# Attention keys in chunks of 128 and a half chunk, natural token order, and one cluster of attention work per head pair

## The chip, the cores and the metric

The kernel runs on one core of one Trainium2 chip. The metric is the device time of one execution in microseconds (us), the median of several runs. All runs quoted here are in the fast state: the medians of one kernel differ by less than 0.3% between sessions. PE is TensorE's matmul stream (the profile calls each entry of it a record), PEld its weight loads, DVE is VectorE, ACT ScalarE, POOL GpSimd, SP the sync engine, which issues nearly all the transfers here.

## The reference

Eight batches, twelve heads, 448 tokens, head dimension 64, all fp32. Then a SwiGLU feed-forward on 3584 tokens of width 768 with a hidden width of 1536.

```python
q_n, k_n = rmsnorm(q, g_q), rmsnorm(k, g_k)          # q, k, v: (8, 12, 448, 64)
attn = softmax(q_n @ k_n.T / sqrt(64))               # per head
x = (attn @ v) -> (B*S, H*D)                         # 3584 x 768
out = (silu(x @ w_gate) * (x @ w_val)) @ w_out       # w_gate, w_val 768 x 1536, w_out 1536 x 768
```

## The kernel before

Two heads make a pair; there are 48 pairs. The first 12 ("early") come before any long feed-forward stretch; the other 36 ("late") are set among the down-products of a block, 12 to a block. There are four blocks of two batches each; a block first makes its up-products (x times `w_gate` and `w_val`), then its down-products (times `w_out`). The last block has no attention in it. A planner written in Python gives each piece an engine and a guessed time, and fixes each engine's order when the kernel is built; the engines then run in order and wait for each other by semaphores.

A pair's 448 tokens are cut into four chunks of 112, with tokens 4p to 4p+3 on partition p. So q and v come as one DMA each, in pieces of 1 KB, and k as two in pieces of 256 B.

```python
BUFS = dict(
    qk=4, v=2, t=2, QT=2, KT=2, e=4, sums1=1, sums3=1, inv=1, rows=3, st=2, at=2, ss=3, rr=4, ...)

def load(name, key, src):                 # name "qk" (q or k) or "v"
    def emit():
        if src is k:
            x = take(name, key, [R, NJ, 2, D])                        # R = 112, NJ = 4, D = 64
            rows = k[b][2 * c : 2 * c + 2].rearrange("h (p j) d -> p j h d", j=NJ)
            for h in range(2):
                nc.sync.dma_start(x[:, :, h], rows[:, :, h])
        else:
            x = take(name, key, [R, 2, NJ, D])
            nc.sync.dma_start(x.rearrange("p h j d -> p h (j d)"), pair_rows(src, m))
    ...
    return add("SP", 0.9 if src is k else 0.45, when, emit, takes=[(name, key)], kb=224, early=25.0)

def square(x):                            # ACT, for the norm; x = 0 for q, 1 for k
    ...
# ... sums on DVE, the inverse root `rr` and the scaling of q into `t` on POOL ...
def transpose(x):                         # PE: 4 transposes for q, 4 for k
    for j in range(NJ):
        src = tiles["qk", (m, 1)][:, j] if x else tiles["t", m][:, 0, j]
        nc.tensor.transpose(transposed_to(x)[:, ts(j, R)], src.rearrange("p h d -> p (h d)"), ident[0:R, 0:R])

def scores(j):                            # PE: two 64x112 row tiles side by side
    for h in range(2):
        nc.tensor.matmul(st[0:R, h, 0:S], tiles["KT", m][rows, j, :], tiles["QT", m][rows]..., start=True, stop=True)
def exps(j):                              # ACT, reads `st`, writes `e`
    ...
def product(name, lhs, rhs, first, last): # PE: weighted sums and denominators, two 112x64 column tiles
    ...
```

## Time and profile before

| | before |
|---|---|
| median, three runs | 1600.94 us (1597.68 to 1601.45) |
| profiled span | 1598.5 us |
| busy PE / DVE / ACT / POOL | 1568.1 / 789.5 / 429.5 / 683.5 us |
| instructions on PE | 5376 |
| 2nd, 3rd, 4th long run of up-products starts at | 532.25, 919.38, 1306.51 us |

In the timeline of PE each block shows one long unbroken run of products with weights `ws` and stationary `xs` (line L1047 before). The starts of the second, third and fourth are marks; the distance between two marks is one whole steady block with 12 late pairs (387.13 us before). The time up to the first mark holds the early stage and block 0. The first marks of the two kernels, before and then after (start, duration, line, shapes, records):

```profile
532.25 171.54 PE L1047 MATMUL mm<-xs,ws 128*128 128x448 f32 x456
```

```profile
573.15 158.01 PE L1076 MATMUL mm<-xs,ws 128*128 128x448 f32 x420
```

### The profile page before, as it was taken

To read this page: it belongs to the slowest core of one execution; us is meant where nothing else is said; L and a number is where in the kernel's file an instruction comes from. 1 tells how busy PE (TensorE), PEld (TensorE's weight loads), DVE (VectorE), ACT (ScalarE), POOL (GpSimd) and SP (SyncE) were. 2 spreads that over 40 slices of the span, in tenths; PEclk is the share of its full clock that TensorE was granted. 3 is DMA by queue.
4 is the path that set the end of the run, shared out by engine and by line. 5 is a ranking of instruction groups with operands and counts; after the bars stand their busy time and mean duration, and the time that the engine had idled before them with its cause. 6 is when DMAs were issued, how large, how long until landed. Compare 5 with 4: busy or idle time off the path is not lost.

```text
span 1598.5 us, 14736 instructions
## 1 busy us (share of the span) xinstructions
PE 1568.1 (98%) x5376; PEld 774.8 (48%) x5376; DVE 789.5 (49%) x873; ACT 429.5 (27%) x689; POOL 683.5 (43%) x440
## 2 busy tenths in 40 slices
PE   6998999999999999999999999999999999999998
PEld 2333555544544555544444455554454445555554
DVE  3999768873554343444454533444344543343221
ACT  6774333334333001123333210103433311000000
POOL 5881356555656213335556422333665632222000
PEclk9999999999999999999999999999999999999999
DMA  5556677622331111212423121213223211111232
GB/s 166 179 162 215 212 246 250 227 83 85 99 120 47 55 59 57 82 61 65 125 76 108 42 69 40 88 55 99 76 81 114 73 59 59 40 59 40 94 109 76
DMA packets 116118, 161.90 MB, mean 101 GB/s; under 512 B 50756, under 2 KB 103236, under 8 KB 112452
## 3 DMA queue, kind: packets, MB, share of 16 engines
q1 hardware_dynamic: 106752, 149.84, 29.4%
q10 hardware_dynamic: 9284, 11.02, 2.3%
q8 instruction: 45, 0.74, 0.2%
q14 instruction: 37, 0.30, 0.1%
HBM read 132.12 MB, written 28.70 MB: 101 GB/s over the span
## 4 chain that ended last, share of the span: by engine, by line
PE 95%; DVE 1%; issue 1%; POOL 1%; ACT 1%; DMA 0%; SPq 0%; POOLq 0%; ACTq 0%; DVEq 0%
PE mm L1047 48%; PE mm L1228 25%; PE at L805 11%; PE st L747 9%; PE st L698 2%; DVE inv L849 1%; POOL rr L666 1%; ACT es L759 1%; PE mm L698 0%; DMA qk<-in_k_dram 0%; DVE xs L884 0%; POOL sums L770 0%; POOL t L679 0%; DVE gt L947 0%; DVE gt L951 0%
## 5 line engine op out<-in xcount | busy, mean ns | idle before, releaser
L1047 PE MATMUL mm<-xs,ws 128*128 128x448 f32 x2016 | 764.9, 541 | 3.8 <-DVE xs L884 3.8
L1047 PEld LDWEIGHTS mm<-xs,ws 128*128 128x128 f32 x2016 | 382.9, 191 | 381.5 <-issue 369.7
L1031 POOL TENSOR_TENSOR ws<-ws 128x384 f32<-128x384 f32 x192 | 200.1, 1053 | 445.3 <-DMA ws<-quarters 326.0
L1228 PE MATMUL mm<-ws,gt 128*128 128x384 f32 x912 | 308.0, 491 | 0.0
L759 ACT ACTIVATE es<-st,rr 112x448 f32<-112x448 f32 x384 | 212.2, 636 | 204.8 <-PE st L747 158.0
L1228 PEld LDWEIGHTS mm<-ws,gt 128*128 128x128 f32 x912 | 168.9, 190 | 136.4 <-issue 27.2
L849 DVE RECIPROCAL inv<-at 128x448 f32<-128x448 f32 x48 | 141.9, 2956 | 101.3 <-PE at L805 101.3
L666 POOL TENSOR_TENSOR rr<-ss,minus_half 112x16 f32<-112x16 f32 x48 | 151.7, 3161 | 83.0 <-DVE ss L658 81.2
L770 POOL TENSOR_TENSOR sums<-es 112x896 f32<-112x896 f32 x48 | 103.7, 2160 | 195.2 <-ACT es L759 133.8
L747 PE MATMUL st<-QT,KT 64*112 64x448 f32 x768 | 174.0, 569 | 6.4 <-ACT es L759 5.2
L773 POOL TENSOR_TENSOR sums<-sums,es 112x896 f32<-112x896 f32 x72 | 151.1, 2098 | 19.5 <-ACT es L759 15.3
L805 PE MATMUL at<-es,v 112*64 112x448 f32 x768 | 154.9, 545 | 2.7 <-DVE inv L849 2.7
L747 PEld LDWEIGHTS st<-QT,KT 64*112 64x112 f32 x768 | 60.9, 174 | 105.0 <-issue 74.3
L1065 DVE TENSOR_TENSOR s<-s,mm 128x448 f32<-128x448 f32 x96 | 59.5, 620 | 103.9 <-PE mm L1047 103.9
L1088 ACT COPY s<-mm 128x448 f32<-128x448 f32 x48 | 25.5, 532 | 293.6 <-PE mm L1047 293.5
L1300 DVE TENSOR_TENSOR rows<-part,mm 128x384 f32<-128x384 f32 x56 | 30.9, 552 | 145.8 <-PE mm L1228 130.2
L1228 PE MATMUL mm<-ws,hs 128*128 128x384 f32 x288 | 97.0, 490 | 0.0
L1065 DVE TENSOR_TENSOR wide<-s,mm 128x448 f32<-128x448 f32 x72 | 44.6, 620 | 101.4 <-PE mm L1047 101.4
L805 PEld LDWEIGHTS at<-es,v 112*64 112x64 f32 x768 | 50.9, 136 | 88.1 <-issue 77.1
L1065 DVE TENSOR_TENSOR gt<-s,mm 128x448 f32<-128x448 f32 x72 | 44.6, 620 | 88.8 <-PE mm L1047 88.8
L1152 ACT ACTIVATE wide<-gt 128x1344 f32<-128x1344 f32 x24 | 31.8, 1326 | 173.3 <-DVE gt L1065 173.3
L638 ACT ACTIVATE t<-qk 112x512 f32<-112x512 f32 x96 | 58.7, 635 | 68.3 <-DMA qk<-in_k_dram 55.0
(70 smaller groups left out, 901.8 us busy)
## 6 DMA issues: line engine op xcount, KB each, us to landing
ws<-quarters SPq DMA_DIRECT2D x48, 768.0 KB, 4.4
ws<-out_sides SPq DMA_DIRECT2D x28, 1152.0 KB, 5.2
qk<-in_q_dram SPq DMA_DIRECT2D x48, 224.0 KB, 4.2
qk<-in_k_dram SPq DMA_DIRECT2D x96, 112.0 KB, 4.0
v<-in_v_dram SPq DMA_DIRECT2D x48, 224.0 KB, 3.0
out_sides<-hs SPq DMA_DIRECT2D x42, 192.0 KB, 6.6
stage<-in_moe_w_val_dram SPq DMA_DIRECT2D x10, 768.0 KB, 6.3
gt<-in_moe_w_gate_dram SPq DMA_DIRECT2D x8, 768.0 KB, 7.0
```

Source lines behind the costliest of these rows:

```text
L638: nc.scalar.activation(tiles["t", m][:, x].rearrange("p j h d -> p (j h d)"), tiles["qk", (m, x)].rearrange("p a b d -> p (a b d)"), AF.Sq ...
L666: nc.gpsimd.tensor_tensor(out=rr, in0=tiles["ss", m], in1=minus_half, op=ALU.pow,)
L747: nc.tensor.matmul(st[0:R, h, 0:S], tiles["KT", m][rows, j, :], tiles["QT", m][rows].rearrange("p j r -> p (j r)"), start=True, stop=True,)
L759: nc.scalar.activation(e[:, h], tiles["st", (m, j)][0:R, h, 0:S], AF.Exp, scale=tiles["rr", m][:, at : at + 1],)
L770: engine.tensor_tensor(out=to, in0=before, in1=e, op=ALU.add)
L773: engine.tensor_tensor(out=to, in0=to, in1=e, op=ALU.add)
L805: nc.tensor.matmul(to[ds(D * h, D), 0:S], lhs(h), rhs[:, h], start=first, stop=last)
L849: nc.vector.reciprocal(inv, tiles[den][:, 0:S])
L1031: lambda to=to, a=a, b=b: nc.gpsimd.tensor_tensor(out=tiles[key][:, to], in0=tiles[key][:, a], in1=tiles[key][:, b], op=ALU.subtract,),
L1047: nc.tensor.matmul(into[:, 0:S], w[:, side, c, :], xs[:, side, c], start=(fresh and c == 0), stop=(c == NK - 1), skip_group_check=not fina ...
L1065: nc.vector.tensor_tensor(out=to(), in0=one(), in1=two[:, 0:S], op=ALU.add)
L1228: nc.tensor.matmul(banks[bank][:, 0:HALF], of(g), w[:, ts(g, HALF)], start=(g == 0), stop=(g == NG - 1),)
```

## The change

The intent: full use of the array for three quarters of the keys (chunks of 128, 128, 128), the last 64 keys by four 64x64 tiles at once, each for half of the queries; tokens in natural order; and the attention steps of a pair in one cluster among the feed-forward products, where many pairs had two (PE's timeline shows 21 clusters of attention in a steady block before). With it the planner's guessed times and some of its constants change, and the output goes out in whole tiles.

Parts of the edit ("..." marks a cut):

```diff
-        qk=4, v=2, t=2, QT=2, KT=2, e=4, sums1=1, sums3=1, inv=1, rows=3, st=2, at=2, ss=3, rr=4,
+        qk=4, v=2, t=2, QT=2, KT=2, e=4, eh=2, sums=1, inv=1, rows=3, st=2, at=1, ss=3, rr=4,
...
-                if src is k:
-                    x = take(name, key, [R, NJ, 2, D])
-                    rows = k[b][2 * c : 2 * c + 2].rearrange("h (p j) d -> p j h d", j=NJ)
-                    for h in range(2):
-                        nc.sync.dma_start(x[:, :, h], rows[:, :, h])
-                else:
-                    x = take(name, key, [R, 2, NJ, D])
-                    nc.sync.dma_start(x.rearrange("p h j d -> p h (j d)"), pair_rows(src, m))
...
+                x = take(name, key, [P, NJ, 2, D])
+                rows = src[b][2 * c : 2 * c + 2].rearrange("h s d -> s h d")
+                for j in range(NJ):
+                    for p in range(0, P, width(j)):
+                        nc.sync.dma_start(x[ds(p, width(j)), j], rows[ds(P * j, width(j))])
+
+            when = ready - (26.0 if name == "qk" else 16.0)
+            return add("SP", 0.9, when, emit, takes=[(name, key)], kb=256, early=25.0)
...
             for j in range(NJ):
                 src = tiles["qk", (m, 1)][:, j] if x else tiles["t", m][:, 0, j]
+                w = width(j)
                 nc.tensor.transpose(
-                    transposed_to(x)[:, ts(j, R)], src.rearrange("p h d -> p (h d)"),
-                    ident[0:R, 0:R],
+                    transposed_to(x)[:, ds(P * j, w)],
+                    src[0:w].rearrange("p h d -> p (h d)"),
+                    ident[0:w, 0:w],
                 )
...
+        for j in (3, 0, 1, 2):
+            when = (ready + 0.3 if j in (3, 0) else base) + 0.01 * (j % 3)
+            half = j == NJ - 1
             st = add(
-                "PE", 0.75, when, lambda j=j: scores(j), after=[kt, qt],
+                "PE", 0.41 if half else 0.76, when, lambda j=j: scores(j), after=[kt, qt],
                 uses=[("KT", m), ("QT", m)], takes=[("st", (m, j))],
-                group=("s", m, j // 2), mode="rows",
-            )
+                group=("c", m - 1 if j in (3, 0) else m), mode="quarters" if half else "rows",
+            )
...
+        def half_product(lhs, at):
+            e = tiles["e", (m, NJ - 1)]
+            for x in range(2):
+                for h in range(2):
+                    nc.tensor.matmul(
+                        tiles["at", m][ds(D * h, D), x, ds(at, Q)], lhs(ds(D * x, D), h),
+                        e[ds(D * x, D), h], start=False, stop=True, skip_group_check=True,
+                    )
```

`width(j)` is 128 for chunks 0 to 2 and 64 for the last, which is loaded twice, to both halves of the partitions. That makes five DMA issues for each of q, k and v, all in pieces of 256 B: 15 a pair, where there were 4.

## The prediction

> **What bounds the kernel now.** I read the busy table and the chain of waits first, to see which engine sets the time.
>
> ```profile
> PE 1568.1 (98%) x5376; PEld 774.8 (48%) x5376; DVE 789.5 (49%) x873; ACT 429.5 (27%) x689; POOL 683.5 (43%) x440
> PE   6998999999999999999999999999999999999998
> PE 95%; DVE 1%; issue 1%; POOL 1%; ACT 1%; DMA 0%; SPq 0%; POOLq 0%; ACTq 0%; DVEq 0%
> ```
>
> TensorE (PE) is busy 98% of 1598.5 us and 95% of the chain. Only the first four slices (160 us), where the first 12 head pairs are made, have holes. So after about 145 us the time is a sum of matmuls, and any PE time saved there is saved whole.
>
> Next the groups of PE instructions (line, operation, shapes, count, then busy us and mean ns), to see how much of that the change touches:
>
> ```profile
> L1047 PE MATMUL mm<-xs,ws 128*128 128x448 f32 x2016 | 764.9, 541 | 3.8 <-DVE xs L884 3.8
> L747 PE MATMUL st<-QT,KT 64*112 64x448 f32 x768 | 174.0, 569 | 6.4 <-ACT es L759 5.2 <-DVE QT L729 0.8
> L805 PE MATMUL at<-es,v 112*64 112x448 f32 x768 | 154.9, 545 | 2.7 <-DVE inv L849 2.7
> L805 PE MATMUL at<-sums,ones 112*64 112x448 f32 x240 | 53.3, 539 | 0.0
> ```
>
> Every fp32 matmul leaves two records. The mean is a latency: the step is shorter. Attention (scores, weighted sums, denominators, transposes) is some 440 us of 1568; the feed-forward products are untouched.
>
> Then the timeline of PE in one late pair (start, duration, line, shapes, records). Starts, not durations, give costs:
>
> ```profile
> 747.19 1.76 PE L747 MATMUL st<-QT,KT 64*112 64x448 f32 x8
> 748.88 3.23 PE L805 MATMUL at<-es,v 112*64 112x448 f32 x16
> 751.94 0.92 PE L805 MATMUL at<-sums,ones 112*64 112x448 f32 x4
> 752.79 1.76 PE L747 MATMUL st<-QT,KT 64*112 64x448 f32 x8
> 754.48 4.14 PE L1228 MATMUL mm<-ws,gt 128*128 128x384 f32 x12
> 758.46 0.55 PE L698 MATMUL st<-ident,qk 112*128 112x112 f32 x4
> 758.84 0.55 PE L698 MATMUL st<-ident,t 112*128 112x112 f32 x4
> 759.23 4.05 PE L1228 MATMUL mm<-ws,gt 128*128 128x384 f32 x12
> ```
>
> Four 112-column transposes take 0.383 us, so 95.75 ns each. In the chain the pure stretches are 189.42 us for 504 records of 448 columns (375.8 ns each) and 96.76 for 300 of 384 (322.5). All three equal 2 x columns / 2.4 + 2.5 ns. Scores at 747.19 take 1.69 for 8 records: two run side by side, 4 x 0.3758 = 1.503, the rest is change of array mode. Whole block check: the product stretches of two successive blocks start at 532.42 and 919.54, 387.12 apart. The order of instructions gives 252 products of 448 (x 0.7517 = 189.4), 150 of 384 (x 0.645 = 96.75), 12 pairs at 8 transposes + 4 score steps + 5 column steps (0.766 + 3.007 + 3.759 = 7.53; x 12 = 90.4), and 57 mode changes. The rest, 10.6 us / 57, is 0.186 us per change.
>
> The early stage, by windows (width, busy of PE, PEld, DVE, ACT, POOL; clock; DMA share; GB/s):
>
> ```profile
> 26.26:80.00 53.74, 50.98 (x270) 20.47 (x270) 45.26 (x38) 44.08 (x73) 43.72 (x19) 1.00 0.52 155
> 80.00:135.20 55.20, 50.47 (x248) 18.66 (x245) 50.59 (x39) 39.54 (x64) 38.42 (x22) 1.00 0.49 158
> ```
>
> PE still leads (101.5 of 108.9 us) but DVE follows at 95.9, ACT at 83.6.
>
> **What the Trainium skill says.** "TensorE: Matmul & The Clock Gate", Wait — 56ns, not 53.3ns?: warm matmuls start N / 2.4 GHz + about 2.5 ns apart. This trace agrees if fp32 counts two cycles per column and record. "TensorEngine Tiling (Array Packing)", Key Properties: going to another tiling mode drains TensorE; here 0.186 us. Same page, Gotcha 1: row tiles may not share a PSUM bank at one time; the change obeys (each query half of the output has its own bank), no run shows it. "DMA: Bandwidth & Descriptors", Specifications: line rate needs at least 512 B per transfer. The trace agrees: at 20 to 23 us 1 KB pieces move at some 370 GB/s, while the 256 B pieces of k move at about 200.
>
> **The change part by part.**
>
> 1. Keys by 128. Per late pair, before: 4 score steps, 4 value steps, 1 denominator step, each 448 wide with two tiles side by side: 9 x 0.7517 = 6.77. After: 3 full chunks of scores, 3 x 0.7517 = 2.26; the last 64 keys as four 64x64 tiles at 224 columns, two records deep: 2 x (2 x 224 / 2.4 + 2.5) = 0.378; the column steps now as two 224-wide halves, 4 x 4 x 0.1892 = 3.03; the half chunk's values 0.378. Sum 6.04, saving 0.73. I don't take all of it: twice as many weight loads (136 ns recorded for 64 columns) must hide behind matmuls half as long, and the author's own schedule now reckons 0.81 per column step and 0.41 per half. I take 0.78 and 0.40: 6.18 with 2.265 for scores, saving about 0.58. Transposes (6 of 128, 2 of 64) keep 0.767.
>
> 2. Clustering. The title suggests fewer mode changes, but the instruction order counts 64 per steady block against 57: full-mode interruptions fall, yet the four-tile mode adds two changes per pair. Cost 7 x 0.186 / 12 = 0.11 per pair. Net 0.47 x 36 late pairs = **17 us**, all on the path. (By the pure formula 22; by the author's step costs about 11.)
>
> 3. Early pairs. Before 6 column steps: 8.28 per pair with transposes; after 7.35, since both values and ones use the half chunk. 12 changes more in the stage: 0.19 per pair. PE saves 0.74 x 12 = 9 us. The second A-side product moves ahead of the one that waits for odd tokens: 2.27 us of work falls into the 2.75 us hole before 135.20. Against it: DVE work is the same, and the order even puts three more weight conversions (about 3.7 us) ahead of the last reciprocal; with 95.9 of 108.9 already used I expect new PE waits of 4 to 5 us.
>
> 4. Loads. q and v go from 1 KB to 256 B pieces, rows are 512 for 448, and a pair needs 15 DMA issues rather than 4. Issue time: k's two took 1.23 us, q 0.33, so 4.6 us per pair (estimate) against 1.9 on SP; transfer at 19 to 20 ns per 256 B (from 35 to 37 us, 885 packets under 512 B and 128 of 1 KB filled 68% of 16 engines; at 44 ns per 1 KB, from 370 GB/s, 18 ns remain for each small one, and 44 to 46 us gives 20) makes 3.7 against 2.3 us per pair. With pairs every 9 us both stay below the limit, but the first keys come about 1.2 us later. Net early gain **5 us**.
>
> 5. ACT, POOL, stores. The half chunk's exp is 224 wide: from 636 ns at 448 and 1326 at 1344 the slope gives about 0.44, so 4.7 us rather than 5.1 per pair; POOL's sums stay. Whole-tile stores halve the output DMAs; tail 0.5 us. None is on the path otherwise.
>
> 1600.9 - 17 - 5 - 0.5 = **1578.5 us**.
>
> **Rivals.** (a) Weight loading binds in the 224-wide and four-tile work. For: loads double while the stream time doesn't. Against: transposes load 128 columns every 95.75 ns though the record lasts 141, so loads pipeline. If the half chunk took twice 0.378, 0.7 us more per late pair and 1.1 early would go: about 1617, a loss; if only the column steps took 0.85, 4 x 0.07 x 48 pairs = 13 us: 1592. (b) DVE becomes the bound early: its loop (sums 1.08, reciprocal 2.95, division 0.62) sits between one pair's output and the next, because the output tile has one buffer. For: 95.9 of 108.9 us. Then early gains nothing: 1583. (c) Loads bind early, SP or DMA: landings stretch to 8.7 us beside weights already; the early stage could lose 5 us: 1588. (d) Everything fits as by formula and early waits don't grow: 1569.
>
> **Range and chances.** The late part lies between 11 and 22 us of gain, early between -3 and +10, so 1566 to 1591. Over 2% faster means below 1568.9, which needs (d) nearly whole: 0.12. Slower by 2% needs several rivals at once: 0.01. Within 2%: 0.87.
>
> **What would show it.** Steady block spacing, 387.1 now, should be about 381.5 (379.7 by formula, 383.4 by the author's costs). In the PE timeline, 16 column matmuls (32 records) should take about 3.1 us, the four-tile groups 0.4 each, changes 0.19. Early, successive weighted sums should be 8.8 to 9.2 us apart, rather than 9.5 to 10; if DVE is the releaser before them, (b) holds; if DMA or SP, (c). First continuous up-products should run from about 140 to 143 us with one product more behind them. Wrong would be: four-tile groups near 0.75, block spacing above 386, or new waits of PE in the late blocks.

## The result, and the profile after

| | before | after |
|---|---|---|
| median | 1601.08 us (1597.68 to 1601.45, 4 runs) | 1660.02 us (1657.10 to 1661.42, 4 runs) |
| ratio | | 1.0371, 95% interval 1.0350 to 1.0392 |
| profiled span | 1598.5 us | 1657.1 us |
| marks | 532.25, 919.38, 1306.51 | 573.15, 968.69, 1365.64 |
| block, from mark to mark | 387.13, 387.13 | 395.54, 396.95 |

A ratio is the mean time of one kernel's runs over the mean of the other's runs in the same rounds, so it isn't quite the ratio of the medians. The changed kernel is slower by 3.7%. The marks say where: 40.9 us are lost before the first mark, 8.4 and 9.8 in the two blocks after it, and nothing in the last block, which has no attention (292.0 us from the last mark to the end before, 291.5 after).

The page of the changed kernel: the busy table, the shares of the chain that ended last, and the count of DMA packets.

```profile
PE 1583.9 (96%) x6576; PEld 839.7 (51%) x6576; DVE 770.0 (46%) x873; ACT 416.9 (25%) x689; POOL 695.7 (42%) x476
...
DMA packets 206629, 166.84 MB, mean 101 GB/s; under 512 B 162756, under 2 KB 193732, under 8 KB 202948
...
PE 73%; POOL 7%; issue 5%; SPq 4%; DMA 4%; DVE 3%; ACT 2%; POOLq 0%; ACTq 0%; DVEq 0%
```

PE is still the busiest engine, but the chain is no longer PE alone: its share fell from 95% to 73%, and POOL, SP's queue (SPq), transfers and "issue" have come in. PE's own busy time rose by 15.8 us, where the prediction had it fall.

The early stage in windows (columns as in the prediction) shows a starved PE:

```profile
26.26:80.00 53.74, 39.72 (x290) 21.04 (x292) 33.11 (x26) 35.06 (x59) 30.88 (x14) 0.84 0.53 136
80.00:135.20 55.20, 47.29 (x386) 25.57 (x380) 42.97 (x38) 36.75 (x66) 37.08 (x17) 0.91 0.58 158
```

In the same 108.94 us PE is busy 87.0 us rather than 101.5, DVE 76.1 rather than 95.9, and the clock, 1.00 before, is 0.84 and 0.91. No engine is near its limit. So something ahead of all of them is late. The timeline of SP, before and then after (start, duration, queue, line, transfer, number of issues), names it:

```profile
0.74 0.40 SPq L623 DMA_DIRECT2D qk<-in_q_dram  x1
1.19 1.39 SPq L620 DMA_DIRECT2D qk<-in_k_dram  x2
...
6.40 1.05 SPq L965 DMA_DIRECT2D gt<-in_moe_w_gate_dram  x2
```

```profile
0.74 2.89 SPq L621 DMA_DIRECT2D qk<-in_q_dram  x5
3.67 3.06 SPq L621 DMA_DIRECT2D qk<-in_k_dram  x5
6.77 2.92 SPq L621 DMA_DIRECT2D v<-in_v_dram  x5
...
18.61 1.18 SPq L994 DMA_DIRECT2D gt<-in_moe_w_gate_dram  x2
```

Five issues of q, of k or of v take about 2.9 us (0.58 each), so a pair takes 8.8 us of SP. The pairs should have come every 9 us, and SP has the weights to issue as well. The first weights are issued at 18.61 us, not 6.40. Summed over its timeline, SP spends 111 of the first 135 us issuing; before it was 34. In the chain that ended last it has 51% of the first 45 us, and 12% of the time from there to 174 us, so it isn't the only thing that PE waits for.

A late pair in PE's timeline (start, duration, line, shapes, records):

```profile
794.73 2.49 PE L821 MATMUL at<-es,v 128*64 128x224 f32 x24
797.05 0.93 PE L821 MATMUL at<-sums,ones 128*64 128x224 f32 x8
797.91 0.61 PE L830 MATMUL at<-eh,v 64*64 64x224 f32 x8
...
803.75 0.69 PE L695 MATMUL st<-ident,qk 128*128 128x128 f32 x4
804.37 0.75 PE L695 MATMUL st<-ident,t 128*128 128x128 f32 x4
805.05 4.14 PE L1262 MATMUL mm<-ws,gt 128*128 128x384 f32 x12
```

By starts, the 32 column records take 3.18 us and the four-tile group 0.43: as predicted. The two groups of transposes take 0.62 and 0.68, where they took 0.383 each: 0.53 us a pair more. The row prints one shape for the group, but the last transpose of each has 64 partitions, not 128.

In other pairs PE also stands still. The same view 40 us later:

```profile
846.35 0.61 PE L830 MATMUL at<-eh,v 64*64 64x224 f32 x8
849.48 0.84 PE L748 MATMUL st<-QT,KT 64*64 64x224 f32 x8 [2.52 <-ACT es L762]
850.53 1.86 PE L748 MATMUL st<-QT,KT 64*128 64x448 f32 x4 [0.20 <-ACT es L762]
852.32 6.22 PE L1262 MATMUL mm<-ws,hs 128*128 128x384 f32 x12
```

The bracket is the idle time before the instruction and what ended it: PE waited 2.52 us until the exps (ACT's exponentials of the scores) had freed a score buffer. After it the same 12 records of down-products take 6.22 us instead of 4.14. The window from 849 to 859 us (columns as above) has a granted clock of 0.66:

```profile
849.00:859.00 10.00, 9.32 (x29) 4.49 (x29) 4.79 (x5) 3.37 (x7) 8.78 (x5) 0.66 0.15 34
```

From the first scores of the cluster to the next transposes this pair takes 16.90 us (841.47 to 858.37), the undisturbed one 10.73 (793.02 to 803.75). Two waits of 2.72 us together so cost 6.2.

So there were three suspects: the issue time of SP (early), the transposes of 64 partitions (all pairs), and waits of PE for ACT (early and late). ACT's table of waits says what ACT itself waits for, before and after (total us, times, longest us):

```profile
ACT t L638 <- DMA qk<-in_k_dram: 55.0, 17, 4.8
```

```profile
ACT t L634 <- DMA qk<-in_k_dram: 147.7, 33, 9.8
```

The Square of k, an ACT instruction, waits 2.7 times as long for its load, and what stands behind it in ACT's order waits too.

### The profile page after: what moved, and what is told of

It reads as the page before. It is cut to its first block, busy times and chain, and to the rows that moved or that the text cites. A ratio compares the mean times of both kernels' runs of the same rounds, so it can differ in the third digit from the quotient of the medians.

```text
span 1657.1 us, 17863 instructions
## 1 busy us (share of the span) xinstructions
PE 1583.9 (96%) x6576; PEld 839.7 (51%) x6576; DVE 770.0 (46%) x873; ACT 416.9 (25%) x689; POOL 695.7 (42%) x476
## 4 chain that ended last, share of the span: by engine, by line
PE 73%; POOL 7%; issue 5%; SPq 4%; DMA 4%; DVE 3%; ACT 2%; POOLq 0%; ACTq 0%; DVEq 0%
PE mm L1076 44%; PE mm L1262 17%; PE at L821 5%; PE st L748 5%; SPq L621 4%; DMA qk<-in_k_dram 3%; POOL sums L775 2%; ACT es L762 2%; POOL sums L772 2%; POOL sums L779 1%; PE st L695 1%; POOL t L675 1%; DVE inv L877 1%; PE at L830 1%; POOL rr L662 1%
## 5 line engine op out<-in xcount | busy, mean ns | idle before, releaser
L662 POOL TENSOR_TENSOR rr<-ss,minus_half 128x16 f32<-128x16 f32 x48 | 146.3, 3047 | 238.7 <-DVE ss L654 237.9
L748 PE MATMUL st<-QT,KT 64*128 64x448 f32 (+1 forms) x960 | 174.9, 523 | 37.2 <-ACT es L762 29.8
L762 ACT ACTIVATE es<-st,rr 128x448 f32<-128x448 f32 x288 | 161.6, 633 | 120.3 <-PE at L821 95.6
L821 PE MATMUL at<-es,v 128*64 128x224 f32 x1152 | 119.6, 357 | 2.8 <-issue 1.5
L748 PEld LDWEIGHTS st<-QT,KT 64*128 64x128 f32 (+1 forms) x960 | 65.1, 176 | 110.3 <-ACT es L762 48.6
L775 POOL TENSOR_TENSOR sums<-sums,es 128x896 f32<-128x896 f32 x48 | 100.6, 2096 | 30.0 <-DVE sums L772 25.9
L772 POOL TENSOR_TENSOR sums<-es 128x896 f32<-128x896 f32 x36 | 75.2, 2088 | 82.3 <-ACT es L762 82.3
L821 PEld LDWEIGHTS at<-es,v 128*64 128x64 f32 x1152 | 78.8, 137 | 54.1 <-issue 21.7
L634 ACT ACTIVATE t<-qk 128x512 f32<-128x512 f32 x96 | 59.3, 632 | 166.9 <-DMA qk<-in_k_dram 147.7
L779 POOL TENSOR_TENSOR sums<-sums,eh 64x448 f32<-64x448 f32 x72 | 91.3, 1268 | 5.5
```

Source lines behind the costliest of these rows:

```text
L662: nc.gpsimd.tensor_tensor(out=rr, in0=tiles["ss", m], in1=minus_half, op=ALU.pow,)
L748: nc.tensor.matmul(st[ds(p, w), h, 0 : S * w // P], tiles["KT", m][rows, ds(P * j, w)], tiles["QT", m][rows, queries], start=True, stop=True,)
L762: nc.scalar.activation(e[:, h], tiles["st", (m, j)][:, h, 0:n], AF.Exp, scale=tiles["rr", m][:, at : at + 1],)
L772: engine.tensor_tensor(out=to, in0=tiles["e", (m, 0)], in1=e, op=ALU.add)
L775: engine.tensor_tensor(out=to, in0=to, in1=e, op=ALU.add)
L779: engine.tensor_tensor(out=to, in0=to, in1=e[ds(D * x, D)], op=ALU.add)
```

## The experiments

Fourteen kernels were run, each against the kernel before in the same rounds.

### 1. Transposes over the whole width

Shortened:

```diff
-                    transposed_to(x)[:, ds(P * j, w)],
-                    src[0:w].rearrange("p h d -> p (h d)"), ident[0:w, 0:w],
+                    transposed_to(x, TB)[:, ts(j, P)], src.rearrange("p h d -> p (h d)"), ident
```

The half chunk is on both halves of the partitions anyway, so the transpose of all 128 only writes 64 columns that nobody reads.

> The changed kernel with one edit: the half chunk's two transposes read all 128 partitions (their rows are there twice) instead of 64, so they stay in the full-array mode. Theory A (the 64-row transposes are a mode change of their own): in the late blocks each group of four transposes falls from 0.63 and 0.68 us to about 0.44, some 0.5 us per pair, 36 pairs, so about 17 to 19 us off 1660: 1641 to 1643. Rival (128-wide transposes are slow in themselves): the groups stay at 0.6 and the time at 1660.

Measured: 1647.41 us, ratio 1.0295 (1.0278 to 1.0313); 12.6 us better than the changed kernel, where 17 to 19 were expected. The groups of transposes take 0.44 us, as the theory said. The blocks are 392.3 and 392.1. PE's wait for exps before its scores rose from 29.8 to 36.8 us, so part of the gain turned into waiting. The transposes are a cause, and not the only one.

### 2. Fewer issues: 10 a pair

The first 384 tokens go three to a partition (pieces of 768 B for q and v); q and v then take 3 issues and k 4, and the transposes write strided columns to restore the order.

```diff
+                    nc.sync.dma_start(
+                        x[:, :, 0 : NJ - 1].rearrange("p h j d -> p h (j d)"),
+                        rows[:, 0:full].rearrange("h (p j) d -> p h (j d)", p=P))
+                for to in last:      # the half chunk, to partitions 0 to 63 and 64 to 127
+                    nc.sync.dma_start(to, rows[:, ds(full, D)].rearrange("h p d -> p h d"))
```

> The changed kernel with the loads alone altered: q and v in 3 DMA issues each and k in 4, by giving partition p the tokens 3p to 3p+2 (768 B runs; the query transposes write strided columns, so outputs stay in natural order): 10 issues per pair instead of 15. Theory B (SP needs about 0.5 us per issue, 8.8 us per pair, and so sets the pace of the early stage and of the late stalls): the first weights' load is issued at about 12 us rather than 18.6, the first weighted sum runs near 32 us rather than 41, the last early one 15 to 20 us earlier, the late stalls before scores (about 4 us of idle in 720 to 880) mostly go: 1625 to 1638. Rival (the waits come from the new order of the cluster, or from DMA bandwidth): the SP share falls but PE still waits, 1650 or more.

Measured: 1641.77 us, ratio 1.0257 (1.0240 to 1.0275): 18 us better, but short of what was expected. The first mark comes at 559.71, 13.4 earlier than in the changed kernel; the blocks stay at 394.9 and 394.3.

### 3. Both

> Both edits together. If the two causes are independent and explain the loss, the gains add: about 1605 to 1620. If one is only the shadow of the other, less than the sum.

Measured: 1633.97 us, ratio 1.0214 (1.0197 to 1.0231). This was a miss: 26 us of 59 mended, not 40 to 55. An undisturbed late pair now takes 15.57 us by its timeline, half a microsecond less than before, yet the blocks are still 392.3 and 391.5. A third cause had to be there.

### 4. The kernel before with 15 issues a pair

Its own layout and order of tokens, but each load in five issues of pieces of 256 B.

```diff
+                for j, lo, hi in ((0, 0, R), (1, 0, R), (2, 0, R), (3, 0, D), (3, D, R)):
+                    nc.sync.dma_start(to[lo:hi, j], rows[lo:hi, j])
```

> The kernel before, with nothing changed but the loads: each of q, k and v in 5 issues of 256 B pieces, as many as the changed kernel has. Theory B: SP then spends 8 to 9 us per pair here too; the start waits for the first keys and the stretch of up-products starts 10 to 25 us later than 145.4: 1612 to 1626. Rival (the number of issues doesn't matter, the new attention order does): 1600 to 1604.

Measured: 1630.19 us, ratio 1.0188 (1.0171 to 1.0205): 30 us lost by the loads alone, more than expected. The first mark is at 562.25 (532.25 before); the blocks are 387.13 and 387.13, exactly as before. So the loads cost only before the first mark here, and what is lost in the late blocks of the changed kernel must have another cause than the loads by themselves.

### 5. Issue count or packet size: two attempts

Experiment 4 changed both. So the kernel before was given 15 issues of its own pieces (1 KB for q and v) by cutting each load along the partitions.

> The kernel before with its own pieces (1 KB for q and v, 256 B for k), its own bytes and layout, but each load cut by partitions into 5 issues, 15 a pair rather than 4. Issue theory: the time follows the count of issues, so it loses as much as the version with 15 issues of 256 B pieces did: 1622 to 1635 us, all of it before the first long product stretch ends. Packet theory (small pieces cost the time): 1600 to 1606.

Measured: 1971.74 us, ratio 1.2323 (1.2300 to 1.2346). The experiment was spoiled by its cuts at 23 and 38 partitions: five issues of q took 4.94 us (0.99 each) and five of k 7.89 (1.58 each). The Trainium skill states ("DMA: Bandwidth & Descriptors", "Why a DMA increments its semaphore by 16 and not by 1") that a transfer is spread over the largest number of DMA engines, at most 16, that divides the outer dimension of both its sides; by that rule 23 partitions go to one engine. The profile doesn't list engines per transfer, so no run here shows that rule itself; the issue times fit with outer dimensions mattering. I made the cuts at multiples of 16:

> The version before with 15 issues of its own large pieces, cut at multiples of 16 partitions (the cuts at 23 and 38 cost 1.0 and 1.6 us an issue and spoiled that run: 1972 us). If an issue again costs some 0.4 to 0.65, the issue theory says it loses as the 15 issues of small pieces did: 1620 to 1640 us, all early; the packet theory says 1600 to 1606.

Measured: 1636.01 us, ratio 1.0226 (1.0209 to 1.0243), inside what the issue theory said. SP's timeline of this run:

```profile
0.74 2.28 SPq L624 DMA_DIRECT2D qk<-in_q_dram  x5
3.06 3.29 SPq L620 DMA_DIRECT2D qk<-in_k_dram  x5
```

With the bytes and pieces of the kernel before, 15 issues lose 36.6 us; with small pieces they lost 30. The first marks, 564.41 and 562.25, lie close together. So the count of issues is the cost here, not the size of the pieces; the time of one issue isn't a constant, though, as the spoiled run shows. (The blocks of this run are 390.0 and 389.3, 2 to 3 us above before; I didn't look for the reason.)

### 6. What the third cause is

A stall in the version of experiment 3, seen in four timelines. PE waits 3.05 us for the exps:

```profile
436.01 2.92 PE L762 MATMUL st<-QT,KT 64*64 64x224 f32 x12 [3.05 <-ACT es L776]
```

ACT did nothing in that time: the exps (434.81) are in order behind the Square of k, which waited 9.42 us for k's load:

```profile
434.28 0.63 ACT L648 ACTIVATE t<-qk 128x512 f32<-128x512 f32 x1 [9.42 <-DMA qk<-in_k_dram]
434.81 2.19 ACT L776 ACTIVATE es<-st,rr 128x448 f32<-128x448 f32 x4
```

SP issued that load only at 430.06, and POOL's scaling of q (into `t`), which frees a raw buffer, ended at 428.99 + 1.04 = 430.03:

```profile
430.06 1.23 SPq L622 DMA_DIRECT2D qk<-in_k_dram  x2
```

```profile
424.37 4.54 POOL L793 TENSOR_TENSOR sums<-sums,eh 64x448 f32<-64x448 f32 x2
428.99 1.04 POOL L689 TENSOR_TENSOR t<-qk,rr 128x512 f32<-128x512 f32 x1
```

So the loop closes through four engines: POOL frees the buffer late, the load starts late and takes 2.5 us to issue and some 1.7 more to land, ACT's Square waits for it, the exps wait behind the Square, and PE waits for the exps, since the four score steps of the cluster share two score buffers (`st=2` in the code; no run gave it more). The first edit that follows cuts the loop at the buffer: it gives the raw q and k a fifth one; a row buffer of the output is given up for the space.

```diff
-        qk=4, v=2, ..., rows=3, ...
+        qk=5, v=2, ..., rows=2, ...
```

> The combined version (whole-width transposes, 10 load issues a pair, 1634 us) with a fifth buffer for raw q and k; a row buffer of the output is given up for the space. Buffer theory: the late stalls come because the load of k may start only when POOL's scaling has freed a buffer, and its Square then stands before the exps in ACT's order; with a fifth buffer both Squares find their data, the long waits of PE for exps in the late blocks go, and a steady block falls from 392 to about 380 to 383, the total to 1597 to 1608 us. Rival 1 (the clustering itself: four score groups on two score buffers, paced by the exps, or POOL's sum of the half chunk): the blocks stay above 388, the total above 1622. Rival 2 (the loss of one row buffer costs something): new waits before the output rows.

Measured: 1594.06 us, ratio 0.9960 (0.9942 to 0.9979), even below the expected range. The blocks are 382.53 and 382.54. Over the whole run PE's wait for exps before its scores is 4.8 us, where it was 35.8 in experiment 3. The late cluster shown here has no wait left. ACT and then PE in this version:

```profile
430.24 1.15 ACT L648 ACTIVATE t<-qk 128x512 f32<-128x512 f32 x2
436.35 2.21 ACT L776 ACTIVATE es<-st,rr 128x448 f32<-128x448 f32 x4 [4.96 <-PE at L835]
```

```profile
428.74 0.60 PE L713 MATMUL st<-ident,qk 128*128 128x128 f32 x4
429.17 0.60 PE L713 MATMUL st<-ident,t 128*128 128x128 f32 x4
429.61 4.04 PE L1276 MATMUL mm<-ws,hs 128*128 128x384 f32 x12
433.57 1.77 PE L762 MATMUL st<-QT,KT 64*128 64x448 f32 x8
```

Both Squares run together as soon as ACT comes to them, and the exps wait for PE, which is as it should be. The groups of transposes take 0.43 and 0.44.

The second edit leaves the buffers and tells the planner the measured issue time of a load (2.0 us rather than 0.9), so that it may put the exps ahead of the Square by itself:

> The combined version with one number changed: the scheduler reckons a load at 2.0 us of the sync engine rather than 0.9 (10 issues were measured at 5.5 to 6.3 us a pair, so 1.8 to 2.1 a load). No instruction is added or removed, only their order. Order theory: the plan put ACT's Square ahead of exps because it believed the data there sooner than it comes; with the true time the stalls shrink: total 1605 to 1622. If only the buffer counts, the Square still waits: 1628 to 1640.

Measured: 1633.22 us, ratio 1.0199 (1.0174 to 1.0224): no change from experiment 3. A better number in the plan didn't help; the buffer did. But this is no test of the order: ACT's timeline of this run shows k's Square still right ahead of the exps in the late blocks, waiting for its load (9.46 us before 435.12), so the new number moved nothing there. Whether exps set ahead of the Square would do without the fifth buffer isn't shown. Both edits together:

> Both edits: if the fifth buffer alone has cured the late blocks, the true issue time can only help in the early stage: 1590 to 1605 us, late blocks as with the fifth buffer alone. If each cures a part, this is better than both by over 5 us.

Measured: 1598.55 us, ratio 0.9987 (0.9966 to 1.0007): the blocks are 382.5 again, but the first mark is at 539.73, 4.3 us later than with the buffer alone. The true issue time even made the early order worse.

Control: the fifth buffer in the kernel before.

> Control: the kernel before with the same two buffer counts. Its Squares too stand behind the load of k, but its exps come in two groups a pair and PE waits for none of them in late blocks, so I expect no gain there: 387.1 per block, total 1595 to 1604. If it gains 5 us or more, the fifth buffer is an improvement apart from the change, and the comparison of the mended version has to be made with this kernel.

Measured: 1600.87 us, ratio 1.0009 (0.9993 to 1.0026). It gains nothing there, so the buffer isn't an improvement apart from the change: the change made it necessary. Which part of the change did so isn't told apart: 15 issues alone left the old blocks at 387.13 (experiment 4), but no run has the new order with 4 issues and four buffers.

### 7. The changed kernel with the fifth buffer alone

> The changed kernel itself with only the fifth raw q and k buffer (and one row buffer less): 15 issues and the half-array transposes stay. If the three causes (issue time, half-array transposes, load waits through too few buffers) add up, a steady block is 382.5 (measured with all three mended) + 12 x 0.54 for the transposes = 389, and the total 1594 + 12.6 (what mending the transposes was worth) + 18 (what fewer issues were worth) = 1625, range 1615 to 1633. If the fifth buffer only works once the issues are fewer, it stays above 1645.

Measured: 1633.95 us, ratio 1.0212 (1.0195 to 1.0229): the buffer alone is worth 26 us. The blocks are 388.71 and 388.72, against the 389 expected, so in the late blocks the 12 x 0.54 us of the transposes are what remains. The total is 9 us over my sum and just outside the stated range; since the blocks are as expected, the 9 us lie before the first mark (563.90).

### 8. What is left in the early stage

With all three mended (1594 us) the first mark is 535.44, still 3.2 later than before, though the steady blocks are 4.6 shorter. Either the 10 issues or DVE, which is busy 38.1 of the 40 us from 120 to 160 us, could be the reason. A first try moved the first load of v behind the second pair's q and k:

> An attempt to beat both: whole-width transposes, 10 issues, fifth buffer (1594.1 us), and the first load of v moved behind the second pair's q and k. The second k should land about 2 us earlier than 13.1, the first weighted sum come 1 to 2 us earlier; DVE, busy 38.1 of the last 40 us of the early stage, may take the gain back. 1589 to 1595 us.

Measured: 1594.08 us, ratio 0.9964 (0.9948 to 0.9981): no gain. Then the loads were made in 4 issues a pair, as in the kernel before. This brings wrong tokens into the half chunk (the result is wrong, with a relative error of 1.45); all other instructions stay.

> Wrong results on purpose: the mended version with v later (1594.1 us), its loads made as in the kernel before, 4 issues a pair in 1 KB and 256 B pieces, which brings wrong tokens into the half chunk but leaves every other instruction. If issues still set the early stage: the first long product stretch of the second block begins at 523 to 529 us (535 to 538 with 10 issues, 532.4 before), the total is 1579 to 1587, what the prediction said. If VectorE sets it (rival b): start above 532, total above 1590.

Measured: 1582.86 us, ratio 0.9896 (0.9876 to 0.9916). The first mark is 524.65 and the blocks are 382.53. So issues still set the early stage at 10 a pair, and DVE (rival b) doesn't. (The pieces of q and v grow to 1 KB as well; experiment 5 speaks against these as the reason.) Last, a correct version: the first two v loads go out from ACT, which is idle at the start.

```diff
+                issue = nc.scalar if name == "v" and m < 2 else nc.sync
-                    nc.sync.dma_start(
+                    issue.dma_start(
```

> Right results: the mended version with the first two v loads issued by ACT, which has little to do in the first 15 us, rather than by the sync engine. Six issues (some 3.7 us) leave the sync queue before the second pair's keys and the first weights. If the start is what is left of the issue cost, 3 to 6 us come off: 1588 to 1592; if the pace later or VectorE sets the end of the stage, it stays at 1593 to 1596.

Measured: 1589.36 us (1586.21 to 1593.04), ratio 0.9928 (0.9901 to 0.9954). The first weighted sum starts at 26.23 us rather than 30.53. This is the fastest correct version here: by the medians 4.3% below the changed kernel, and 0.7% faster than the kernel before, which is clear of the noise but small. Against the 1594.06 us without this edit the gain is likely and not certain: the two were run in different sessions, and the intervals of their ratios overlap.

## Why the prediction was wrong, point by point

| version | median | first mark | block |
|---|---|---|---|
| before | 1600 | 532.25 | 387.1 |
| after | 1660 | 573.15 | 395.5, 397.0 |
| after, fifth buffer | 1634 | 563.90 | 388.7 |
| and whole-width transposes, 10 issues | 1594 | 535.44 | 382.5 |
| and 4 issues (wrong data) | 1583 | 524.65 | 382.5 |

The prediction had given 0.01 to a loss of over 2%. Two of its own signs of being wrong came: blocks above 386 (395.5 and 397.0), and new waits of PE in the late blocks (9.4 us for exps between the first and the last mark, none before). Its premise that after about 145 us the time is a sum of matmuls held for the kernel before and not for the changed one.

- **Step 1, the matmuls.** Right where it counted streams: the column group took 3.18 us, the four-tile groups 0.43, so rival (a), weight loads that bind, didn't come. The term that failed is "Transposes (6 of 128, 2 of 64) keep 0.767": they took 1.30 a pair. Experiment 1 shows that the 64-partition transposes were the reason: over the whole width a group falls from 0.62 and 0.68 to 0.43 and 0.44. I had written in the same text that another tiling mode drains the array and that a change costs 0.186 us, and didn't see that a transpose of 64 partitions is one. That this drain is the mechanism is argued, not shown: twice two changes at 0.186 would be 0.74 (an estimate), of which 0.53 shows. In the steady block it costs 388.7 - 382.5 = 6.2 us; 0.53 x 36 late pairs makes some 19 us (an estimate).
- **Step 2, clustering.** The net saving held: with the causes mended a block is 4.6 us shorter, against the 5.6 predicted; full-width transposes at 0.87 a pair rather than 0.767 are about the difference of 1 us (0.1 x 12). The mode changes weren't counted in a trace. What the step missed is what the cluster waits for. In the cluster four groups of scores share two score buffers, so PE cannot run past exps that are late. Before, ACT waited 55 us for k and PE only 5.2 us for exps before its scores; after, PE's wait there is 29.8 us, and a stretch of lower clock follows the longer ones. "I expect new PE waits of 4 to 5 us" was said of DVE and the early stage only. The fifth buffer alone gave back 26 us.
- **Step 3, the early stage.** DVE wasn't the bound: with 4 issues a pair the first mark came 7.6 us earlier than before, of which 4.6 belong to block 0, if it gained as the steady blocks did, and 3 to the early stage (5 were predicted). The sign of the step was right; the loads had hidden it.
- **Step 4, loads.** This is the largest miss. I sized the issue time as 4.6 us a pair, and the step doesn't show how. Its own reading of k, 1.23 us for two issues, gives 15 x 0.615 = 9.2; measured were 0.58 each, 8.8 us a pair. "With pairs every 9 us both stay below the limit" failed: with the weights, SP issued for 111 of the first 135 us, and each wait for a buffer holds up all that stand behind it. The first pair's keys were all issued at 6.73 us rather than 2.58, 4.2 us later and not 1.2. In the kernel before, 15 issues cost 30 us (small pieces) and 36.6 us (its own pieces). Rival (c) named SP, but put it at 5 us and 1588.
- **Step 5, ACT, POOL and stores.** From the last mark to the end of the span before takes 292.0 us and after 291.5. That is near the spread: versions with the old stores take 291.7 to 292.0, those with the new ones 291.3 to 291.8. "None is on the path otherwise" failed: POOL's share of the chain rose from 1% to 7%, and in the stall of experiment 6 its scaling of q is what frees the buffer late.
- **Sums.** Small slips changed nothing: the last sum gives 1578.4, the parts of the range give 1568 to 1592, the slope gives 0.46 us for the half exp and not 0.44 (0.448 was measured), and in the window of "about 200" GB/s (44 to 46 us) a quarter of the packets are not small ones.

The three causes together are more than the loss: the buffer 26 us, transposes with 5 issues of 15 another 40 (1634 to 1594), the other 6 issues 11, which is 77 us down to 1583. They don't simply add: before the buffer was there, transposes and 5 issues were worth 26 us together (1660 to 1634), after it 40. The version with 4 issues, which computes wrong results, lies 18 us below the kernel before of its session, of the 22.4 predicted. So most of the gain that was predicted was there, and three costs that were left out or mis-sized buried it.

What stays open: whether the clock would have fallen without the waits ahead of it (all stretches of lower clock that I looked at follow a wait), how the 40 us of 1634 to 1594 split exactly between transposes and issues (the marks put 6.2 in each of two steady blocks and 28.5 before the first mark), whether the cluster needs the fifth buffer with 4 issues, with more score buffers or with another order on ACT, and whether a correct layout with 4 issues exists.

## What to carry to other kernels

Count the DMA issues of a change, not only its bytes, and multiply by the time of one issue read from the issuing engine's own timeline; when that comes near the pace of the loop, the engine that issues can become the bound, even though the table of busy times doesn't list it. When work is gathered into one cluster, follow each wait in it back through every in-order engine to the buffer that releases it: a buffer count that was enough for spread work can stop the main engine. Keep an auxiliary operation, here a transpose, in the tiling mode of its neighbours, even if that means computing columns that nobody reads.

## What the Trainium skill lacked or had wrong

- "DMA: Bandwidth & Descriptors", "Issuing engines are not separate DMA queues", says that the time on the sequencer to initiate a DMA is "usually small relative to the DMA itself". Here a transfer of the changed kernel costs mostly 0.47 to 0.61 us of the sync engine, of some 2.2 us to landing, and with 15 a pair the sync engine issued for 111 of the first 135 us; in the mended version, issuing six early ones from ACT went with 4.7 us less (1594.06 to 1589.36, in different sessions).
- The same page, "Why a DMA increments its semaphore by 16 and not by 1", tells how the outer dimension sets the number of engines; this section says nothing of the time to issue, which moved with it: 0.46 us for q cut at multiples of 16 partitions and 0.99 cut at 23; 0.66 for k cut at multiples of 16 and 1.58 cut at 38, 76 and 56; the kernel with the odd cuts took 23% longer.
- "TensorEngine Tiling (Array Packing)", Key Properties, has the drain but no figure (0.186 us per change by the count in the prediction), and doesn't warn of a transpose of 64 partitions between others of 128, which I take to pay it: groups of four took 0.62 and 0.68 us rather than 0.43 and 0.44.
- "TensorE: Matmul & The Clock Gate", "Why this matters for your kernels", asks for no idle gaps over about 3 us. Here a wait of 2.52 us was followed by 10 us at a mean granted clock of 0.66.
